# Windowed attention with a gated FFN on one core: DMA transposes issued one chunk earlier, loads reordered, a mask built on VectorE

## The chip, the core and the metric

The kernel runs on one core of a Trainium2 chip. The metric is the device time of one execution in microseconds (us). A profile is one execution recorded by the hardware profiler; its span is 1.7 to 1.8 us shorter than the time of the same run. Engines are called TensorE (PE in the profile, PEld for its weight loads), VectorE (DVE), ScalarE (ACT), GpSimd (POOL) and SP, which only issues DMAs here. In profile lines, `qn` and `kn` are q and k of a chunk as loaded, `qT` and `kT` the same transposed, `xb` the attention output and `xT` its transpose, `uu` and `hT` VectorE's two steps of the gate, `ost` a piece of output before its store, and `ps` a bank of PSUM, which the matmuls here write to.

## The reference, cut to what matters

Attention with 8 batches, 8 heads, 576 positions and head size 64; a query sees the 64 latest keys, itself included. Its output is laid out as 4608 tokens x 512 and goes through a gated FFN with 1536 inner columns.

```python
rel = pos[:, None] - pos[None, :]
mask = (rel >= 0) & (rel < 64)
scores = np.where(mask, scale * q @ k.T, -1e9)
attn = softmax(scores)
x = (attn @ v) as (4608, 512)
g = x @ w_gate
out = (g / (1 + exp(-g)) * (x @ w_val)) @ w_out
```

## The kernel before

The tokens are worked through in 36 chunks of 128 for attention and 9 chunks of 512 for the FFN. Every operation is recorded in program order, and the waits are derived from what it reads and writes. The parts that matter, cut and slightly simplified:

GpSimd issues all loads, in program order. q and k of chunk n go to one of 6 buffers, so a load waits until the chunk 6 back has been transposed. q and k of chunks 4 to 7 are transposed by TensorE (`T`), those of chunk 8 and later by DMA transposes that SP issues (`TD`). The attention output `xb` is transposed for the FFN in the same two ways (`X`, `XD`).

```python
W(2, 4)
self.init_mask(self.mask, "mask", 0.0)       # 4 selects on GpSimd
self.init_va(4, self.NV, "pool")             # 6 memsets on GpSimd
for f in range(4, 12, 2):
    W(f, f + 2)                              # W slices, gate and value
for n in range(4, 8):
    load(n)                                  # q, k, v of chunk n
...
for f in range(6):
    self.F(0, f, 256, 512)
self.T(4)                                    # TensorE needs q, k of chunk 4
...
self.S(8)
self.TD(10)
self.O(0, 0)                                 # ends in an output store on SP
...
def block(n):
    load(n + 5)
    self.A(n, n + 1)                         # attention of n, with the scores S(n + 1) inside
    if n != 11:
        self.XD(n)                           # xb -> xT by DMA transpose
    self.TD(n + 3)                           # q, k of chunk n + 3 by DMA transpose
```

Blocks 8 to 11 fall into FFN chunk 1. The first matmuls of FFN chunk 2, `F(2, 0)`, need xT of chunks 8 to 11; that of chunk 11 is made by TensorE.

The softmax here doesn't subtract the row's maximum and nothing guards it: scores larger than these inputs give would overflow.

Of the kernel before, what the change touches and what calls it, by code (L numbers as in the profile page):

```python
# [5 lines left out]
ALU = mybir.AluOpType  # L6
# [4 lines left out]
NCH = T // 128  # L11
# [138 lines left out]
class _Kernel:  # L150
# [70 lines left out]

    def init(self):
        g = self.g
        ident, mask = self.ident, self.mask
        g.op("dve", lambda e: e.memset(self.wz[:, :], 0.0), writes=["wz"])  # L225
        g.op("dve", lambda e: e.memset(ident[:, :], 0.0), writes=["ident"])  # L226
        g.op("dve", lambda e: e.memset(self.nmask[:, :], 0.0), writes=["nmask"])
        g.op("dve", lambda e: e.memset(mask[:, :], 1.0), writes=["mask"])
        g.op("dve", lambda e: e.memset(self.wup[:, :], 0.0), writes=["wup"])
        g.op("act", lambda e: e.activation(self.wup[:, :], self.wup[:, :], ACTF.Exp), writes=["wup"])  # L230
        g.op("dve", lambda e: e.memset(self.kT[:, :, 0:64], 0.0), writes=[("kT", -1, p) for p in range(4)])
        self.init_va(0, 4)

    def init_va(self, i0, i1, eng="dve"):
        g = self.g
        for i in range(i0, i1):
            va = self.va[i]
            g.op(eng, lambda e, va=va: e.memset(va[:, :, 64:80], 1.0), writes=[("va", i)],
                 after=[self.last_sel] if eng == "pool" else [])

    def init_pool_a(self):
        ident = self.ident
# [1 line left out]
            out=ident[:, :], in_=ident[:, :], compare_op=ALU.not_equal, fill=1.0, base=0,  # L244
            pattern=[[-1, 128]], channel_multiplier=1), writes=["ident"])

    def init_mask(self, m, key, fill):
        for p0, c0, op in ((0, 0, ALU.is_ge), (0, 64, ALU.is_gt), (64, 0, ALU.is_gt), (64, 64, ALU.is_ge)):
            d = m[p0:p0 + 64, c0:c0 + 64]
            sg = 1 if op == ALU.is_gt else -1  # L250
            self.last_sel = self.g.op("pool", lambda e, d=d, op=op, sg=sg: e.affine_select(  # L251
                out=d, in_=d, compare_op=op, fill=fill, base=0,
                pattern=[[-sg, 64]], channel_multiplier=sg), writes=[key])

    def load_qk(self, n):
        i = n % self.NQ
# [317 lines left out]
    def build(self):  # L574
        W = lambda a, b: (self.load_w("g", a, b), self.load_w("v", a, b))

        def load(n):
            if n < NCH:
                self.load_qk(n)
                self.load_v(n)  # L580

        self.first_loads()
        self.init()
        self.load_v(0)
        self.init_pool_a()
        self.load_v(1)
        self.init_mask(self.nmask, "nmask", -30000.0)
        W(0, 1)
        self.load_qk(2)
        W(1, 2)  # L590
        self.load_qk(3)
        self.load_v(2)
        self.load_v(3)
        W(2, 4)
        self.init_mask(self.mask, "mask", 0.0)
        self.init_va(4, self.NV, "pool")
        for f in range(4, 12, 2):
            W(f, f + 2)
        for n in range(4, 8):
            load(n)  # L600

        self.banks("a", [5, 6, 7, 4, 0, 1])
        self.warm(13)
        self.first_cast("k", None, "dve")
        self.first_cast("q", 0, "act")
        self.first_cast("q", 1, "dve")
        tk = self.first_T("k")
        tq = self.first_T("q")
        b0, b1 = self.bias(0), self.bias(1)
        for n in range(2):  # L610
            self.first_ev("k", n, "dve", *tk)
            self.first_ev("q", n, "act", *tq)
        self.S(0, b0)
        self.S(1, b1)
        self.warm(4)
        self.A(0)
        self.warm(2)
        self.A(1)
        self.warm(1)
        self.X(0, "act")  # L620
        self.warm(3)
        self.X(1, "act")
        self.warm(2)
        self.banks("a", [5, 6, 7, 4])
        self.F(0, 0, 0, 256)
        self.F(0, 1, 0, 256)
        self.T(2, "dve")
        self.T(3, "dve")
        load(8)
        b2 = self.bias(2)  # L630
        self.S(2, b2)
        b3 = self.bias(3)
        self.S(3, b3)
        self.F(0, 2, 0, 256)
        self.A(2)
        self.A(3)
        self.F(0, 3, 0, 256)
        self.X(2, "act")
        self.F(0, 4, 0, 256)
        self.X(3, "act")  # L640
        self.F(0, 5, 0, 256)
        self.load_wo(0, 6)
        self.load_wo(6, 12)
        load(9)

        for f in range(6):
            self.F(0, f, 256, 512)
        self.T(4)
        load(10)
        self.F(0, 6)  # L650
        self.S(4)
        self.T(5)
        load(11)
        self.F(0, 7)
        self.A(4, 5)
        self.F(0, 8)
        self.T(6)
        load(12)
        self.X(4, "act")
        self.F(0, 9)  # L660
        self.A(5, 6)
        self.F(0, 10)
        self.T(7)
        self.X(5, "act")
        self.F(0, 11)
        self.A(6, 7)
        self.TD(8)
        self.F(1, 0, 0, 256)
        self.F(1, 1, 0, 256)
        self.X(6, "act")  # L670
        self.F(1, 2, 0, 256)
        self.A(7)
        self.TD(9)
        self.F(1, 3, 0, 256)
        self.F(1, 4, 0, 256)
        self.X(7, "act")
        self.F(1, 5, 0, 256)
        for f in range(3):
            self.F(1, f, 256, 512)
        self.S(8)  # L680
        self.TD(10)
        self.O(0, 0)
        for f in range(3, 6):
            self.F(1, f, 256, 512)

        def block(n):
            if n >= NCH:
                return
            load(n + 5)
            self.A(n, n + 1 if n + 1 < NCH else None)  # L690
            if n != 11:
                self.XD(n)
            if n + 3 < NCH:
                self.TD(n + 3)

        place = {(1, 1, 2): 8, (1, 2, 0): 9, (1, 2, 1): 10, (1, 3, 0): 11,
                 (2, 0, 0): 12, (2, 1, 0): 13, (2, 1, 2): 14, (2, 2, 1): 15, (2, 3, 0): 16}
        for n in range(17, NCH):
            place[(n - 5) // 4, (n - 5) % 4, 0] = n
        for c in range(1, NFC):  # L700
            for u in range(int(c == 1), 4):
                late = c == NFC - 1 and u == 3
                for s in range(3):
                    if (c, u) != (1, 1):
                        self.F(c, 3 * u + s)
                    if s != 1 and (c, u, s) in place:
                        block(place[c, u, s])
                    if s == 1 and not late:
                        self.O(c - 1, u)
                    if s == 1 and (c, u, s) in place:  # L710
                        block(place[c, u, s])
                    if (c, u, s) == (1, 3, 1):
                        self.X(11, "act")
                if late:
                    self.O(c - 1, u)
        for u in range(3):
            self.O(NFC - 1, u)
        self.O_last(NFC - 1, 3)
        self.g.emit()
# [42 lines left out]
```

## Time and profile before

The kernel before took 347.3 us (median of 3, 346.23 to 348.19).

| stretch of the profile | what TensorE does |
|---|---|
| 0 to 31 us | first chunks, short gaps |
| 31.4 to 34.5 | waits for k of chunk 4 |
| 34.8 to 38.2 | works at half clock |
| 79.0 to 84.15 | waits for qT of chunk 11 |
| 84.15 to 89.4 | works at half clock |
| 97.6 to the end | FFN chunk 2 and later, busy throughout: 249.44 us |

The page divides the span into 40 slices; each digit is a busy share in tenths, and PEclk is the granted TensorE clock. From the page of the kernel before:

```profile
PE   6986998994999999999999999999999999999996
...
PEclk9999899997899999999999999999999999999999
DMA  9999999999999999999999999992333211100012
```

After the first quarter TensorE has no gap. The DMA engines are full for the first 27 slices. The gaps by their releaser, from the view of TensorE's waits (engine, line, what it waited for: us in total, times, longest):

```profile
PE ps L394 <- DMA qT<-qn: 5.1, 1, 5.1
PE ps L350 <- DMA kn<-in_k_dram: 3.0, 1, 3.0
...
PE ps L394 <- ACT ost L544: 0.9, 2, 0.4
PE ps L508 <- DVE uu L516: 0.6, 1, 0.6
```

L394 are the matmuls of the scores, L350 TensorE's transposes of q and k, L508 the first matmuls of the FFN (one line lower each in the changed kernel). Two waits hold nearly all of it. Around them, the busy times in stretches of 2 us (columns: PE, PEld, DVE, ACT, POOL busy, granted clock, DMA share, GB/s):

```profile
34.00:36.00 2.00, 1.54 (x11) 0.99 (x12) 0.00 (x0) 0.75 (x2) 2.00 (x4) 0.70 2.43 159
36.00:38.00 2.00, 2.00 (x7) 0.61 (x5) 0.42 (x1) 0.93 (x2) 2.00 (x4) 0.50 2.43 155
...
82.00:84.00 2.00, 0.00 (x0) 0.00 (x0) 0.00 (x0) 0.00 (x0) 0.00 (x0) 0.65 1.53 152
84.00:86.00 2.00, 1.85 (x43) 1.19 (x44) 0.87 (x4) 1.08 (x2) 1.65 (x2) 0.50 1.39 161
86.00:88.00 2.00, 2.00 (x6) 0.70 (x5) 1.42 (x4) 0.60 (x1) 2.00 (x4) 0.50 1.46 150
```

Each of these two waits costs its own time and then a stretch at half clock, in which TensorE shows as fully busy but does about half the work: four matmuls of 512 columns take 1.78 to 1.91 us there, and 1.03 at full clock. The chain of waits shows why qT of chunk 11 came so late (start, duration, what):

```profile
66.67 8.82 DMA kn<-in_k_dram
75.49 8.57 DMA qT<-qn
84.06 0.09 issue
84.15 0.59 PE ps L394 x10
```

The transpose was issued at 75.49 and landed at 84.06. Late in the kernel, where the DMA engines have little to do, the same transpose lands about 2.5 us after its issue.

### The profile page before, as it was taken

Reading aid. Unit: us, or ns where it says so; the run is one execution under the profiler, and the core shown is the slowest. Engines: PE = TensorE matmul, PEld = TensorE weight load, DVE = VectorE, ACT = ScalarE, POOL = GpSimd, SP = SyncE. Lnnn points to the kernel's source line nnn. Section 1 sums busy time; section 2 is a strip of 40 time slices with the busy share of each in tenths; the row PEclk is TensorE's granted clock in tenths of the full one; section 3 lists DMA queues with packets and bytes.
Section 4 is the critical chain, followed back from the end, with each engine's and each line's share of the span. In section 5 each row is a group of like instructions: output and inputs, shape, how many; then the busy total and the mean of one; then the engine's idle time right before and its main releaser. Section 6 shows DMA issues by size and latency. Waiting matters only on the chain.

```text
span 347.1 us, 8322 instructions
## 1 busy us (share of the span) xinstructions
PE 330.0 (95%) x3489; PEld 166.4 (48%) x3489; DVE 212.6 (61%) x465; ACT 139.2 (40%) x252; POOL 112.7 (32%) x151
## 2 busy tenths in 40 slices
PE   6986998994999999999999999999999999999996
PEld 3565457642444444444444444444444444444444
DVE  4366489661666676666666666666666666555520
ACT  2562674441344454444444444444444442232321
POOL 7999995322363436333331633300000000000000
PEclk9999899997899999999999999999999999999999
DMA  9999999999999999999999999992333211100012
GB/s 173 146 179 178 155 202 141 152 190 153 158 105 123 152 135 149 132 130 121 129 118 119 125 130 126 127 122 77 77 77 77 60 47 52 55 30 32 31 47 105
DMA packets 169909, 40.26 MB, mean 116 GB/s; under 512 B 156432, under 2 KB 165392, under 8 KB 169872
## 3 DMA queue, kind: packets, MB, share of 16 engines
q0 software_dynamic: 117312, 18.36, 76.0%
q1 hardware_dynamic: 51376, 20.72, 30.9%
q10 hardware_dynamic: 1184, 0.66, 0.7%
q8 instruction: 27, 0.44, 0.5%
q14 instruction: 10, 0.08, 0.1%
HBM read 37.75 MB, written 9.44 MB: 136 GB/s over the span
## 4 chain that ended last, share of the span: by engine, by line
PE 75%; POOL 11%; DMA 10%; issue 3%; DVE 0%; ACT 0%; POOLq 0%
PE ps L508 45%; PE ps L532 24%; DMA qn<-in_q_dram 5%; PE ps L443 3%; POOL va L325 3%; DMA kn<-in_k_dram 3%; DMA qT<-qn 2%; POOL kn L263 2%; PE ps L394 2%; POOL qn L263 2%; POOL Wv L331 2%; POOL Wg L331 2%; PE ps L561 1%; POOL Wo L336 0%; POOL nmask L251 0%
## 5 line engine op out<-in xcount | busy, mean ns | idle before, releaser
L516 DVE SCALAR_TENSOR_TENSOR uu<-sig,ps 128x512 bf16<-128x512 bf16 (+1 forms) x120 | 75.9, 632 | 91.9 <-ACT sig L514 91.7
L508 PE MATMUL ps<-xT,Wg 128*128 128x512 bf16 (+1 forms) x480 | 115.6, 364 | 0.9 <-DVE uu L516 0.6
L508 PE MATMUL ps<-xT,Wv 128*128 128x512 bf16 (+1 forms) x480 | 114.6, 362 | 0.4 <-DMA Wv<-in_moe_w_val_dram 0.4
L532 PE MATMUL ps<-Wo,hT 128*128 128x512 bf16 x420 | 95.9, 379 | 0.0
L514 ACT ACTIVATE sig<-ps 128x512 bf16<-128x512 f32 (+1 forms) x120 | 66.6, 555 | 62.6 <-PE ps L508 62.2
L518 DVE SCALAR_TENSOR_TENSOR hT<-uu,ps 128x512 bf16<-128x512 bf16 (+1 forms) x120 | 76.0, 634 | 4.9 <-PE ps L508 0.8
L508 PEld LDWEIGHTS ps<-xT,Wv 128*128 128x128 bf16 x480 | 47.2, 99 | 48.5 <-issue 2.2
L263 POOL DMA_DIRECT2D qn<-in_q_dram x38 | 34.3, 915 | 105.6 <-DMA qT<-qn 105.3
L532 PEld LDWEIGHTS ps<-Wo,hT 128*128 128x128 bf16 x420 | 41.0, 98 | 49.1
L508 PEld LDWEIGHTS ps<-xT,Wg 128*128 128x128 bf16 x480 | 44.1, 99 | 42.5 <-issue 2.2
L544 ACT ACTIVATE ost<-ps 128x512 f32<-128x512 f32 x35 | 20.9, 597 | 95.9 <-PE ps L532 95.9
L404 ACT ACTIVATE pt<-ps 128x512 bf16<-128x512 f32 x72 | 38.9, 595 | 29.3 <-PE ps L394 28.7
L325 POOL DMA_DIRECT2D va<-in_v_dram x40 | 36.4, 919 | 1.7 <-DVE ident L226 0.8
L263 POOL DMA_DIRECT2D kn<-in_k_dram x38 | 34.6, 915 | 3.1 <-DMA Wo<-in_moe_w_out_dram 3.1
L461 DVE TENSOR_TENSOR xb<-ps,rc 128x256 bf16<-128x256 f32 x72 | 30.6, 425 | 2.5
L409 DVE TENSOR_TENSOR pt<-pt,mask 128x512 bf16<-128x512 bf16 x64 | 24.2, 417 | 0.5 <-ACT pt L404 0.4
L443 PE MATMUL ps<-va,pt 64*64 64x65 bf16 x1088 | 23.0, 197 | 0.6 <-DVE pt L409 0.2
L443 PEld LDWEIGHTS ps<-va,pt 64*64 64x64 bf16 x1088 | 15.3, 107 | 15.8 <-issue 11.2
L458 DVE RECIPROCAL rc<-ps 128x4 f32<-128x4 f32 x72 | 12.6, 175 | 15.6 <-PE ps L443 15.6
L394 PE MATMUL ps<-qT,kT 64*64 64x64 bf16 (+1 forms) x864 | 16.1, 203 | 6.0 <-DMA qT<-qn 5.1
L394 PEld LDWEIGHTS ps<-qT,kT 64*64 64x64 bf16 x864 | 12.8, 109 | 8.5 <-issue 7.0
L311 PE MATMUL ps<-wz 128*128 128x512 bf16 x25 | 7.8, 446 | 1.3 <-DVE wz L225 1.3
(44 smaller groups left out, 62.8 us busy)
## 6 DMA issues: line engine op xcount, KB each, us to landing
out_dram<-ost SPq DMA_DIRECT2D x35, 256.0 KB, 2.5
va<-in_v_dram POOLq DMA_DIRECT2D x32, 128.0 KB, 6.2
qn<-in_q_dram POOLq DMA_DIRECT2D x30, 128.0 KB, 4.5
kn<-in_k_dram POOLq DMA_DIRECT2D x30, 128.0 KB, 6.0
Wo<-in_moe_w_out_dram POOLq DMA_DIRECT2D x2, 768.0 KB, 14.0
Wg<-in_moe_w_gate_dram POOLq DMA_DIRECT2D x5, 256.0 KB, 6.3
Wv<-in_moe_w_val_dram POOLq DMA_DIRECT2D x5, 256.0 KB, 7.1
fq<-in_q_dram ACTq DMA_DIRECT2D x1, 512.0 KB, 6.0
```

The costliest lines, as they stand in the source:

```text
L263: self.g.op("pool", lambda e, d=d, a=a: e.dma_start(d, a), writes=ks, dma=True)
L325: g.op("pool", lambda e, d=d, a=a: e.dma_start(d, a), writes=ks, dma=True)
L394: r = e.matmul(sv[h][o:o + 64, c, q0:q1], self.kT[ps, c, kk:kk + 64], qT[ps, c, q0:q1], start=not biased, stop=not biased or c == 3 and kk ...
L404: g.op("act", lambda e, po=po, si=si: e.activation(po, si, ACTF.Exp, scale=SCALE), reads=[bk], writes=[pk])
L409: "dve", lambda e: e.tensor_tensor(po, po, m, ALU.mult), reads=[pk, "mask"], writes=[pk]))
L443: r = e.matmul(av[half][ws, j, :], pt[ks, h, ws], vv[ks, h, 0:65], start=key == q[0], stop=key == q[-1])
L461: g.op("dve", lambda e, xo=xo, rb=rb, a=av[half]: e.tensor_tensor(xo, a[:, :, 0:64], rb, ALU.mult), reads=[bk, ("rc", ir)], writes=[("xb", ...
L508: r = e.matmul(bank[:, 0:n], W[:, kk, f * 128:f * 128 + 128], xT[:, kk, t0:t1], start=(kk == 0), stop=(kk == NK - 1))
L514: g.op("act", lambda e: e.activation(sig[:, 0:n], G[:, 0:n], ACTF.Tanh, scale=0.5), reads=[gk], writes=[("sig", i)])
L516: g.op("dve", lambda e: e.scalar_tensor_tensor(uu[:, 0:n], sig[:, 0:n], 1.0, G[:, 0:n], ALU.add, ALU.mult), reads=[("sig", i), gk], writes ...
L518: g.op("dve", lambda e: e.scalar_tensor_tensor(hT[:, f, t0:t1], uu[:, 0:n], 0.5, V[:, 0:n], ALU.mult, ALU.mult), reads=[("uu", i), vk], wr ...
L532: r = e.matmul(OB[:, :], hT[:, f, 128 * u:128 * u + 128], self.Wo[:, f, :], start=(f == 0), stop=(f == NF - 1))
```

## The change

Its intent: take away both waits. Loads of chunks 4 and 5 go between the W slices. Chunk 11 is transposed right after chunk 10, ahead of the output stores, and each block transposes four chunks ahead instead of three, with loads six ahead. The multiplicative mask comes from the additive one by one comparison on VectorE, and the six memsets move there too, which frees GpSimd for issuing loads.

```diff
-        self.init_va(0, 4)
+        self.init_va(0, self.NV)
...
-    def init_mask(self, m, key, fill):
+    def init_mask(self):
...
+        self.g.op("dve", lambda e: e.tensor_scalar(self.mask[:, :], self.nmask[:, :], -1.0, None, ALU.is_ge),
+                  reads=["nmask"], writes=["mask"])
...
-        W(2, 4)
-        self.init_mask(self.mask, "mask", 0.0)
-        self.init_va(4, self.NV, "pool")
-        for f in range(4, 12, 2):
+        for f in range(2, 8, 2):
             W(f, f + 2)
-        for n in range(4, 8):
-            load(n)
+        self.load_qk(4)
+        W(8, 10)
+        self.load_v(4)
+        load(5)
+        W(10, 12)
+        load(6)
+        load(7)
...
         self.TD(10)
+        load(13)
+        self.TD(11)
         self.O(0, 0)
...
-            load(n + 5)
+            load(n + 6)
...
-            if n + 3 < NCH:
-                self.TD(n + 3)
+            if n + 4 < NCH:
+                self.TD(n + 4)
```

(All ten memsets of `init_va` are on VectorE now. `init_mask` builds the additive mask on GpSimd as before and then derives the other. The memset of the old mask and the arguments that are no longer used go too.)

More of the change, by code (lines that the diff above doesn't have):

```diff
@@ L223, in init @@
         g = self.g
-        ident, mask = self.ident, self.mask
+        ident = self.ident
         g.op("dve", lambda e: e.memset(self.wz[:, :], 0.0), writes=["wz"])
@@ L227, in init @@
         g.op("dve", lambda e: e.memset(self.nmask[:, :], 0.0), writes=["nmask"])
-        g.op("dve", lambda e: e.memset(mask[:, :], 1.0), writes=["mask"])
         g.op("dve", lambda e: e.memset(self.wup[:, :], 0.0), writes=["wup"])
@@ L231, in init, with init_va @@
         g.op("dve", lambda e: e.memset(self.kT[:, :, 0:64], 0.0), writes=[("kT", -1, p) for p in range(4)])
-        self.init_va(0, 4)
-    def init_va(self, i0, i1, eng="dve"):
-        g = self.g
+        self.init_va(0, self.NV)
+    def init_va(self, i0, i1):
         for i in range(i0, i1):
             va = self.va[i]
-            g.op(eng, lambda e, va=va: e.memset(va[:, :, 64:80], 1.0), writes=[("va", i)],
-                 after=[self.last_sel] if eng == "pool" else [])
+            self.g.op("dve", lambda e, va=va: e.memset(va[:, :, 64:80], 1.0), writes=[("va", i)])
     def init_pool_a(self):
@@ L245, in init_pool_a @@
             pattern=[[-1, 128]], channel_multiplier=1), writes=["ident"])
-    def init_mask(self, m, key, fill):
+    def init_mask(self):
         for p0, c0, op in ((0, 0, ALU.is_ge), (0, 64, ALU.is_gt), (64, 0, ALU.is_gt), (64, 64, ALU.is_ge)):
-            d = m[p0:p0 + 64, c0:c0 + 64]
+            d = self.nmask[p0:p0 + 64, c0:c0 + 64]
             sg = 1 if op == ALU.is_gt else -1
-            self.last_sel = self.g.op("pool", lambda e, d=d, op=op, sg=sg: e.affine_select(
-                out=d, in_=d, compare_op=op, fill=fill, base=0,
-                pattern=[[-sg, 64]], channel_multiplier=sg), writes=[key])
+            self.g.op("pool", lambda e, d=d, op=op, sg=sg: e.affine_select(
+                out=d, in_=d, compare_op=op, fill=-30000.0, base=0,
+                pattern=[[-sg, 64]], channel_multiplier=sg), writes=["nmask"])
+        self.g.op("dve", lambda e: e.tensor_scalar(self.mask[:, :], self.nmask[:, :], -1.0, None, ALU.is_ge),
+                  reads=["nmask"], writes=["mask"])
     def load_qk(self, n):
@@ L586, in build @@
         self.load_v(1)
-        self.init_mask(self.nmask, "nmask", -30000.0)
+        self.init_mask()
         W(0, 1)
```

## The prediction

> **What bounds it.** The span is 347.1 us. From about 90 us to the end TensorE is the limit: the table by stretch shows it busy in practically every microsecond, and the chain of waits is matmuls alone. The change removes no TensorE work, so it can only gain before 90 us. There the waits of TensorE show two stalls worth naming:
>
> 1. 3.0 us at 31.4-34.5, waiting for kn of chunk 4. Its load is queued behind all W slices; loads of that stage come about 9 us after their issue, in issue order, so it is throughput of the DMA engines that decides, not issue time. The granted clock is 0.5 for 3.4 us afterwards (0.70 and 0.50 in the 2 us stretches from 34), which costs about 1.7 us more. Together 4.7.
> 2. 5.1 us at 79.0-84.15, waiting for the DMA transpose qT of chunk 11, issued at 75.5 and landed at 84.06: 8.6 us under a full load queue, where the same transpose late in the kernel takes about 2.4. The clock is 0.5 until 89.5, another 2.7. Together 7.8 to 7.9.
>
> The Trainium skill ("TensorE: Matmul & The Clock Gate", Part 1) gives half rate after an idle window of about 3.4 us; this trace agrees, the 0.6 us gap at 54 us cost no clock.
>
> **What the change does.** The order of loads: of the W slices, four loads (8 to 11, about 1.35 us of queue each) go behind chunk 4's q and k, so these should land near 29 instead of 34.4; stall 1 goes. But the queue's total is the same: chunk 5's k (near 34.4) and chunk 6's k (near 39.5, unmoved) are now wanted near 34.2 and 38.9 by a TensorE that is 4.7 us earlier. I leave 0.7 us of stall there.
>
> Chunk 11's transposes move from behind block 8 to behind chunk 10's: issued when kn lands, near 63.7, landed near 71-73, wanted near 74.3. Stall 2 goes. Chunk 12's (landed near 78) are wanted near 78.5, and chunk 10's xT (near 84) by the first matmuls of FFN chunk 2, near 84: no slack. "DMA: Bandwidth & Descriptors" (Issuing engines are not separate DMA queues) says that all queues share the 16 engines; the trace agrees: transposes and loads interleave there from 61 to 96 us. I leave 1 us of new stalls, too short to halve the clock.
>
> "Loads six ahead" changes little by itself: the GpSimd queue has the same order of loads and is held by the buffers' readers (105 us of waits for qT), so earlier transposes free it.
>
> Mask on VectorE: takes 2.1 us of GpSimd time (15.2-17.3), adds under 1 us of VectorE memsets near 2 us, where it waits for fk until 5.9. The DMA queue is 5 us behind issue there, so I count 0.
>
> **Sum.** 347.3 - (4.7 - 0.7) - (7.9 - 1.0) = 336.4 us. Range 333.9 to 340.5. Chances: faster 0.88, same 0.11, slower 0.01.
>
> **What would show it.** TensorE's wait for kn near 31 us under 1 us, no half clock after it; no 5 us wait for qT, no half clock near 84; the part from block 12 on unchanged in length, starting about 11 us earlier; the landing of Wo (54.8) unmoved.
>
> **What would make it wrong.** If transposes are held by their share of the engines rather than by latency, chunk 12's qT or chunk 10's xT lands 3 to 5 us late, and the stall moves there and takes the clock with it: 340 to 342. If chunk 5 or 6 lands later than I think, 1 to 2 us come back. If nothing of this binds, 334.5.

## The result, and the profile after

The changed kernel took 338.77 us (median of 4, 338.6 to 339.25), against 347.75 beside it. Ratios here are the mean time of one kernel's runs over that of the other's of the same rounds, so not quite the ratio of the medians quoted: 0.9751, 95% interval 0.9717 to 0.9785. The span is 337.0 us, against 347.1. From its page (its PE row; this trace holds no record of the clock, and that of a second profile of the same kernel, shown below it, stays at full):

```profile
PE   7989989999899999999999999999999999999996
```

```profile
PEclk9999999999999999999999999999999999999999
```

TensorE's waits of the changed kernel:

```profile
PE ps L507 <- DVE hT L517: 1.3, 1, 1.3
PE ps L393 <- ACT ost L543: 1.3, 3, 0.4
...
PE ps L507 <- DVE uu L515: 0.6, 1, 0.6
...
PE ps L393 <- DMA qT<-qn: 0.2, 1, 0.2
```

Both long waits are gone, and a new one of 1.3 us stands at the head of the list. The same stretches as before around the first one, and the new gap:

```profile
34.00:36.00 2.00, 2.00 (x27) 1.15 (x17) 1.70 (x4) 1.84 (x4) 2.00 (x4) 1.00 1.74 182
36.00:38.00 2.00, 2.00 (x55) 1.10 (x54) 1.22 (x2) 1.78 (x4) 2.00 (x4) 1.00 2.38 156
...
86.00:88.00 2.00, 0.69 (x4) 0.22 (x3) 1.38 (x2) 0.04 (x1) 1.00 (x2) 1.00 1.76 154
```

TensorE does the same matmuls in the same order in nearly all kernels, so two positions serve as a ruler: M1, the start of the transposes of xb of chunk 6 (just after the first stage), and M3, the start of `F(2, 0)`. Both are read from the traces.

| kernel | M1 | M1 to M3 | M3 to end | span |
|---|---|---|---|---|
| before | 53.81 | 43.81 | 249.44 | 347.1 |
| changed | 49.06 | 38.52 | 249.43 | 337.0 |
| changed, once more | 49.01 | 38.78 | 249.44 | 337.2 |

The last part is the same to 0.01 us: the whole change in span happens before M3, 4.75 us in the first part and 5.29 in the second.

### The profile page after: what moved, and what is told of

Its sections match the earlier page's. It is cut to its first block, busy times and chain, and to the rows that moved or that the text cites. A ratio compares the mean times of both kernels' runs of the same rounds, so it can differ in the third digit from the quotient of the medians.

```text
span 337.0 us, 8332 instructions
## 1 busy us (share of the span) xinstructions
PE 326.7 (97%) x3489; PEld 165.2 (49%) x3489; DVE 213.3 (63%) x471; ACT 139.1 (41%) x252; POOL 111.0 (33%) x141
## 4 chain that ended last, share of the span: by engine, by line
PE 85%; DMA 5%; POOL 4%; DVE 2%; ACT 1%; issue 1%; SPq 0%; POOLq 0%
PE ps L507 52%; PE ps L531 26%; PE ps L442 3%; DMA Wv<-in_moe_w_val_dram 3%; DMA qT<-qn 3%; PE ps L393 2%; POOL Wg L330 1%; POOL va L324 1%; PE ps L560 1%; POOL Wv L330 1%; DVE uu L515 1%; PE ps L349 1%; ACT ost L543 1%; POOL qn L262 1%; POOL kn L262 1%
## 5 line engine op out<-in xcount | busy, mean ns | idle before, releaser
L507 PE MATMUL ps<-xT,Wg 128*128 128x512 bf16 (+1 forms) x480 | 113.3, 359 | 2.2 <-DVE hT L517 1.3
L507 PE MATMUL ps<-xT,Wv 128*128 128x512 bf16 (+1 forms) x480 | 113.0, 358 | 0.3 <-DMA Wv<-in_moe_w_val_dram 0.2
## 6 DMA issues: line engine op xcount, KB each, us to landing
kn<-in_k_dram POOLq DMA_DIRECT2D x30, 128.0 KB, 10.2
```

Of the source, the lines that this page charges most:

```text
L507: r = e.matmul(bank[:, 0:n], W[:, kk, f * 128:f * 128 + 128], xT[:, kk, t0:t1], start=(kk == 0), stop=(kk == NK - 1))
```

## The experiments

Twelve kernels ran, each with runs of the kernel before on the same chip; all results were correct. The ruler for them:

| run | median us | before beside it | ratio (95%) | M1 | M1 to M3 |
|---|---|---|---|---|---|
| e1_loads | 343.34 | 347.77 | 0.9884 (0.9844 to 0.9924) | 50.17 | 43.32 |
| e2_td | 343.1 | 347.77 | 0.9849 (0.9795 to 0.9904) | 55.16 | 37.88 |
| e3_gate | 344.42 | 347.77 | 0.9902 (0.9856 to 0.9949) | 52.07 | 39.39 |
| e4_poolmask | 339.77 | 347.77 | 0.9781 (0.9742 to 0.982) | 50.23 | 38.26 |
| e6_td11_only | 340.77 | 346.87 | 0.9805 (0.977 to 0.984) | 48.98 | 40.70 |
| e7_x10 | 337.12 | 346.87 | 0.9705 (0.9676 to 0.9734) | 49.06 | 36.88 |
| e8_xd10_first | 337.1 | 346.87 | 0.9709 (0.9676 to 0.9743) | 48.78 | 37.16 |
| e10_warm | 344.8 | 346.87 | 0.9926 (0.989 to 0.9962) | 52.65 | 41.06 |
| e13_after_again | 338.41 | 346.81 | 0.9757 (0.9723 to 0.979) | 49.01 | 38.78 |
| e11_mask_late | 339.09 | 346.81 | 0.9773 (0.974 to 0.9806) | 48.94 | 38.70 |
| e12_mask_only | 345.44 | 346.81 | 0.9972 (0.9929 to 1.0015) | 53.05 | 43.80 |
| e5_load5_late | 342.01 | 346.81 | 0.9853 (0.9808 to 0.9898) | 52.54 | 37.96 |

One question needed no run. "Loads six ahead" with `load(n + 5)` in the blocks, and without the explicit `load(13)`, builds to the same instructions in the same order on every engine as the changed kernel. GpSimd has no other work between loads, so where the load stands in the program changes nothing; the buffers' readers hold it.

### e1_loads: the order of loads alone

```diff
 # kernel before
-        for f in range(4, 12, 2):
+        for f in range(4, 8, 2):
             W(f, f + 2)
-        for n in range(4, 8):
-            load(n)
+        self.load_qk(4); W(8, 10); self.load_v(4); load(5); W(10, 12); load(6); load(7)
```

> The kernel before with the new order of loads alone (mask still on GpSimd, transposes as before). Theory: stall 1 goes with its clock penalty, and TensorE, SP and GpSimd all move about 4.7 us earlier, chunk 11's transposes included, so stall 2 stays as it is: about 342.8 us. Rival: the backlog of loads alone decides when qT of chunk 11 lands (84 us); then stall 2 grows by what stall 1 gave, and the time stays near 347.

343.34 us, as the theory had it. Of TensorE's waits in this run:

```profile
PE ps L394 <- DMA qT<-qn: 4.6, 1, 4.6
...
PE ps L350 <- DMA kn<-in_k_dram: 0.3, 1, 0.3
```

The first wait goes, the second stays, and M1 comes 3.6 us earlier. TensorE starts on qT of chunk 11 at 79.94 instead of 84.15, so the rival, a landing that stays at 84, is out. M1 is 1.1 us later than in the changed kernel, which has the same order of loads; e4 says why.

### e2_td: the earlier transposes alone

```diff
 # kernel before
         self.TD(10)
+        load(13)
+        self.TD(11)
         self.O(0, 0)
-            load(n + 5)
+            load(n + 6)
-            if n + 3 < NCH:
-                self.TD(n + 3)
+            if n + 4 < NCH:
+                self.TD(n + 4)
```

> The kernel before with the earlier transposes alone (chunk 11 ahead of the output stores, four ahead in the blocks). Theory: stall 1 stays (3.0 us and a clock of 0.5 for 3.4 us); stall 2 goes with its clock, 7.2 us; about 340.3, up to 341.6 if the wait for xT of chunk 10 that the changed kernel shows near 87 us comes too. Rival: the two parts need each other, and less than 5 us come: over 342.5.

343.1 us, from 340.85 to 344.22: the median is the rival's number, and the time alone would have decided for it. The profile decides otherwise. It has no wait for qT at all; M1 to M3 takes 37.88 us, 5.9 less than before, even less than in the changed kernel. What was lost lies in the first part: this run waited 3.6 us for k of chunk 4, and the half clock lasted 6.8 us (33.8 to 40.65, so it began within the wait), twice as long as after the first wait in the profile of before.

```profile
PE ps L350 <- DMA kn<-in_k_dram: 3.6, 1, 3.6
PE ps L508 <- DVE uu L516: 1.7, 2, 1.1
```

The second line holds the new wait near 93 us, 1.1 us here. The four runs order by their mean granted clock: 340.85 and 342.51 us at 1.00, 343.7 at 0.995, 344.22 at 0.99. So the two parts don't need each other. That the spread is the clock's is likely for most of it, but not shown: two runs at 1.00 differ by 1.66 us, and 1.00 also stands for profiled runs whose traces hold no record of the clock (the changed kernel, e3).

### e3_gate: is it the full load queue that makes a transpose late?

Nothing is transposed earlier; the load of chunk 14 waits for qT of chunk 11, which leaves the DMA engines a load of 0.3 to 0.6 from 72 to 78 us (the DMA share of the profile), against about 2 in the kernel before.

```diff
 # kernel before
-                self.load_qk(n)
+                self.load_qk(n, [self.last_td] if n == 14 else ())   # last_td: the latest qT transpose
```

> The kernel before, transposes and W slices as they were; only the first load of chunk 14 waits for the landing of qT of chunk 11, so that loads 14 to 16 do not fill the DMA engines from 72 to 84 us. Theory (a full load queue makes a transpose land 8 us after its issue): qT of chunk 11, issued near 75.5, lands within 4 us, stall 2 shrinks to under 1 us: about 340.5 to 341.5. Rival (the transposes are slow by themselves, or by what stands ahead of them on SP): the landing stays 7 to 9 us after the issue, and the time stays near 347 or grows because loads come later.

The view of DMA issues for the two transposes of chunk 11 (the last number is us from issue to landing), in this run and then in the kernel before:

```profile
kT<-kn SPq DMA_TRANSPOSE x1, 4.0
qT<-qn SPq DMA_TRANSPOSE x1, 3.1
```

```profile
kT<-kn SPq DMA_TRANSPOSE x1, 7.8
qT<-qn SPq DMA_TRANSPOSE x1, 8.6
```

That is the theory's answer: 3.1 us instead of 8.6, with the same things ahead of it on SP. Before the scores of chunk 11 TensorE waited only 0.44 us, for a PSUM bank. The time, 344.42, is worse than expected (340.5 to 341.5), because the loads that were held back started at 77 us, and qT of chunk 12, issued at 78.4 among them, landed at 84.6:

```profile
PE ps L394 <- DMA qT<-qn: 2.6, 1, 2.6
```

This one is chunk 12's. The wait moved one chunk on. The trace of e3 holds no record of the clock, but TensorE's pace shows full clock after both of its waits, of 2.63 and 2.57 us (1.03 us for four matmuls of 512 columns). It is the fastest of the four runs, 342.62 us; the other three have mean clocks of 0.99 and 0.995, so some half clock is in the median too. Holding loads back treats the cause, but only for as long as they are held; issuing transposes early leaves the queue full and gives them the time.

### e4_poolmask: the changed kernel with the mask back on GpSimd

```diff
 # changed kernel: init_va, init_mask and the mask's memset as in the kernel before
-        for f in range(2, 8, 2):
-            W(f, f + 2)
+        W(2, 4)
+        self.init_mask(self.mask, "mask", 0.0)
+        self.init_va(4, self.NV, "pool")
+        for f in range(4, 8, 2):
+            W(f, f + 2)
```

> The changed kernel with the mask and the six memsets back on GpSimd behind the slices W 2 and 3. Theory: the queue of loads is 5 us behind its issue there, so 2.1 us of GpSimd time cost nothing: 338.8, within 0.5. Rival: later issue delays every load after it by 2 us, and chunk 6, which lands just when it is wanted, stalls TensorE near 39 us: 340 to 341.

339.77 us: about 1 us slower than the changed kernel (ratio 0.9781 against 0.9751), between the two theories, and outside what I had expected. M1 is 1.2 us later. The intervals of the two ratios overlap; M1 is clearer: in the six traces with the new order of loads for chunks 4 to 7 and no early mask on GpSimd it lies from 48.78 to 49.06, in the two with it at 50.17 and 50.23 (e1, e4). TensorE waits for chunk 5, and then for 0.44 us more at chunk 6:

```profile
PE ps L350 <- DMA kn<-in_k_dram: 0.8, 1, 0.8
```

```profile
40.05 0.38 PE L350 MATMUL ps<-ident,kn 128*128 128x128 bf16 x4 [0.44 <-DVE xb L461]
```

The profile puts the second down to VectorE, but k of chunk 6 landed at 39.96. The two waits together are the 1.2 us.

So my reading that "the DMA queue is 5 us behind issue" was wrong. The packets show it. In the kernel before, the first W load after the 2.1 us gap was issued at 17.28 and, counting packets in order, had its first one at 19.58, 2.3 us later. Thirteen later loads of that kernel found nothing queued ahead of them on GpSimd, and their first packets still came 1.4 to 1.6 us after the issue, their landing 3.3 to 4.3 us after it (97.52, 99.10 and 100.97 for the first of them). So the 5 us from issue to landing were mostly the latency of a load and its own transfer; some 0.7 us were queue. In the changed kernel the corresponding load waited 4.4 us (15.09 to 19.47), so the queue was some 2.8 us there, and the gap used it up but for 0.7. The rate dropped 5 us after the gap: in all six traces with the mask on GpSimd near 15 us it is 136 to 158 GB/s from 22 to 24 us, in the other eight 197 or 198. That the mask there causes the drop is thus shown; why it comes so late, and with 0.7 us still queued, is not. The stretch from 22 to 24 us, in the kernel before, this run and the changed kernel, in that order (last column: GB/s):

```profile
22.00:24.00 2.00, 1.92 (x61) 1.63 (x62) 1.86 (x8) 0.38 (x1) 2.00 (x4) 1.00 1.28 151
```

```profile
22.00:24.00 2.00, 1.59 (x29) 1.20 (x30) 1.86 (x8) 0.38 (x1) 2.00 (x4) 1.00 1.21 136
```

```profile
22.00:24.00 2.00, 1.93 (x61) 1.47 (x58) 1.86 (x8) 0.38 (x1) 2.00 (x4) 1.00 1.45 198
```

### e12_mask_only: the mask on VectorE alone

The kernel before with the new `init_va` and `init_mask`, and nothing else.

> The kernel before with the mask on VectorE alone. Theory: loads after 17 us land about 1 us earlier, so the wait for kn of chunk 4 is about 2 us instead of 3, with the clock as before: about 1 us faster than before, 346 where before is 347. Rival: the queue hides it, no change.

345.44 us against 346.81, a ratio of 0.9972 whose interval includes 1: by time alone no difference is shown. The rate from 22 to 24 us is 197 GB/s, as the theory has it, and the wait for chunk 4 is 0.8 us shorter than before's 3.0, with M1 0.8 us earlier. That shorter wait is no proof by itself: e2 and e3, with the loads of before, waited 3.6 and 2.6 us.

```profile
PE ps L349 <- DMA kn<-in_k_dram: 2.3, 1, 2.3
```

### e11_mask_late: the same GpSimd work where the queue is deep

```diff
 # e4_poolmask
-        self.init_mask(self.mask, "mask", 0.0)      # from behind W(2, 4)
-        self.init_va(4, self.NV, "pool")
...
         load(5)
+        self.init_mask(self.mask, "mask", 0.0)
+        self.init_va(4, self.NV, "pool")
         W(10, 12)
```

> The changed kernel with the mask and memsets back on GpSimd, but 11 us later than before had them: behind chunk 5's loads, near 26 us. Theory (a gap in the issues costs only where loads wait less for the engines than the gap is long): near 15 us a load lands 5 us after its issue, of which some 4 are there without any queue, and the gap of 2 us cost 1 us; near 26 us loads land 9 us after their issue, so the same gap costs nothing: as the changed kernel beside it, within 0.4, and no dip of the DMA rate near 22 or 31 us. Rival (GpSimd time delays all that comes after it, wherever it is): 0.8 to 1 us slower than the changed kernel, as when the mask stood near 15 us.

The dip is gone (198 GB/s from 22 to 24 us, and 150 near 31 us against 151 in the changed kernel), no load is waited for, and M1 is 48.94 us, as in the changed kernel (49.01 beside it). So for the stage in question the gap costs nothing there. The times don't quite follow: 339.09 against 338.41, 0.7 us apart where at most 0.4 was expected, while the two profiled spans are 337.1 and 337.2. The intervals of the two ratios overlap widely. I leave the remainder open.

### e13_after_again: the changed kernel once more

> The changed kernel once more, unedited, as the measure for the three runs beside it on the same chip: 338.8, within 0.5.

338.41 us (338.13 to 339.02, five runs), as expected. Its profile has the new wait at 1.6 us.

### e5_load5_late: only chunk 4 between the W slices

```diff
 # changed kernel
-        load(5)
         W(10, 12)
+        load(5)
```

> The changed kernel with chunk 5's loads back behind all W slices; only chunk 4 stays between them. Theory: kn of chunk 5 lands 2.7 us later, near 36.2, wanted near 34: a wait of about 2 us, and in some runs a slow clock after it: 340.5 to 342.5. Rival: chunk 4 alone was the stall, and the rest has slack: 338.8.

342.01 us, within the theory's range. The wait moved to chunk 5, and a half clock follows it (0.59 in the stretch from 36 us):

```profile
PE ps L349 <- DMA kn<-in_k_dram: 2.1, 1, 2.1
```

```profile
36.00:38.00 2.00, 1.97 (x12) 1.14 (x13) 0.00 (x0) 1.08 (x2) 2.00 (x4) 0.59 2.43 155
```

Once chunk 4 is early, chunk 5 is next in line: each move of a load must be judged with TensorE where it will then be, not where it was.

### e6_td11_only: chunk 11 early, the rest three ahead as before

```diff
 # changed kernel
-            if n + 4 < NCH:
-                self.TD(n + 4)
+            if 11 < n + 3 < NCH:
+                self.TD(n + 3)
```

> The changed kernel with only chunk 11's transposes early: from block 9 on each block issues the transposes of three chunks ahead, as before. Theory: a transpose under the load queue lands 7 to 9 us after its issue, so qT of chunk 12, now issued near 74 instead of 70.8, lands near 82 and is wanted near 79: a new wait of 1.5 to 3 us for it; xT of chunk 10 is issued 2 to 3 us earlier on a freer SP and its wait of 1.3 us goes: 338.5 to 341. Rival: chunk 11 alone mattered and four ahead is an ornament: no wait for qT, 337.5.

340.77 us, within the theory's range. qT of chunk 12 was issued at 73.7 instead of 70.8 and landed at 81.2:

```profile
PE ps L393 <- DMA qT<-qn: 2.2, 1, 2.2
```

Half clock followed for 3.4 us, and the wait near 87 us did not come. Four ahead is needed, for chunk 12.

### e7_x10 and e8_xd10_first: what is the new wait of 1.3 us?

The profile puts it down to VectorE's `hT`. In the timeline of the changed kernel, TensorE starts just as that instruction ends (start, duration, engine, line, what):

```profile
85.24 1.03 PE L507 MATMUL ps<-xT,Wv 128*128 128x512 bf16 x4
...
86.79 0.69 DVE L517 SCALAR_TENSOR_TENSOR hT<-uu,ps 128x512 bf16<-128x512 bf16 x1
87.47 1.19 SPq L362 DMA_TRANSPOSE kT<-kn  x1
...
87.58 1.02 PE L507 MATMUL ps<-xT,Wg 128*128 128x512 bf16 x4 [1.31 <-DVE hT L517]
```

But the DMA transpose of chunk 10's xb landed at 87.38, and these matmuls read it. SP had issued it only at 78.8: chunk 13's two transposes stood ahead of it, and the second held SP from 75.6 to 78.1. Two ways to take that away:

```diff
 # e7_x10: changed kernel, xT of chunk 10 made by TensorE and ScalarE
-            if n != 11:
+            if n not in (10, 11):
                 self.XD(n)
...
+                    if (c, u, s) == (1, 2, 2):
+                        self.X(10, "act")
```

> The changed kernel with xT of chunk 10 made by TensorE and ScalarE, as that of chunk 11 is, instead of by a DMA transpose. Theory: the wait of 1.3 us near 86 us, which the profile puts down to VectorE, is the wait for this transpose (landed 87.4); it goes, against some 0.3 us of TensorE for the four transposes: 337.7. Rival: it is VectorE's hT or a PSUM bank: 338.8 to 339.2.

```diff
 # e8_xd10_first: changed kernel, chunk 13's transposes behind chunk 10's xT
+            if n == 9:
+                return
+            if n == 10:
+                self.TD(13)
             if n + 4 < NCH:
                 self.TD(n + 4)
```

> The changed kernel with the transposes of chunk 13 moved on SP from behind block 9 to behind the DMA transpose of chunk 10's xT in block 10. Theory: SP was held by chunk 13's two transposes (its qT issue took 2.5 us), so xT of chunk 10 is issued near 76 instead of 78.8 and lands near 84, before it is wanted at 86.3; the wait of 1.3 us goes and nothing is added on TensorE: 337.4; chunk 13 is wanted near 87 and lands near 86. Rival: the landing is set by the load queue and not by the issue, and it lands near 87 all the same: 338.8.

337.12 us (337.01 to 337.17) and 337.1 (336.74 to 338.07): both faster than the changed kernel by 1.3 to 1.7 us (338.41 and 338.77; these two did not run beside it), and neither has the wait. In e8 the DMA transpose was issued at 76.3 and landed at 83.7, and TensorE goes on before VectorE's `hT` has even begun:

```profile
85.94 1.03 PE L507 MATMUL ps<-xT,Wg 128*128 128x512 bf16 x4
86.59 0.74 PEld L507 LDWEIGHTS ps<-xT,Wv 128*128 128x128 bf16 x4
86.63 0.69 DVE L517 SCALAR_TENSOR_TENSOR hT<-uu,ps 128x512 bf16<-128x512 bf16 x1
```

The wait was for the DMA transpose; the name in the profile was that of the engine that happened to finish last. In e8 the part from M3 to the end is 249.72 us, 0.28 longer than elsewhere: qT of chunk 13, now behind, landed at 88.14, and its scores start at 88.18. e7, with the narrower spread, is the version to keep: 0.9705 of before.

### e10_warm: waits filled with work, nothing moved

```diff
 # kernel before
             self.F(0, f, 256, 512)
+        self.warm(12)                       # matmuls on zeros
         self.T(4)
...
+            if n == 10:
+                self.warm(22)
             self.A(n, n + 1)
```

> The kernel before with nothing moved: 12 matmuls on zeros (about 0.22 us each) ahead of the transposes of chunk 4 and 22 ahead of block 10, so that TensorE works through most of both waits and its clock stays at full. Theory: each wait costs its own time and then a clock of 0.5 for one or two steps of 3.4 us; the second part goes here, 1.7 to 3.4 us and 2.7 to 3.4 us: 342 to 344, and a narrower spread than before's 346 to 349. Rival: the slow clock hides under other waits and costs nothing; then the time is 347 or more.

344.8 us against 346.87, at the upper end of what was expected, and the four runs lie within 0.44 us (before: 346.21 to 348.65 in its seven). The clock stayed at full. So some 2 us (1.3 to 3.8 by the interval of the ratio) is the least that the half clock cost in the kernel before; the zeros also made TensorE late, as the run waited 1.2 us for a bank ahead of the first of them and had no wait left for chunk 4. This shows the second cost of a wait apart from its first.

## Why the prediction was right, and where its sizes were off

The change made the kernel faster, and the time, 338.77 us, lies in the range of 333.9 to 340.5. It is 2.4 us above the point, 336.4. Point by point:

- **Both named waits were the gain, and nothing after them changed.** Right: both are gone with their half clocks, and from M3 on the two traces agree to 0.01 us.
- **First part: 4.7 less 0.7.** It gave 4.75. The 0.7 of "stall there" did not come, and the reason is the term that the prediction put at zero: "The DMA queue is 5 us behind issue there, so I count 0". Latency was taken for a queue. Without the mask's move chunks 5 and 6 are waited for (e4, 1.2 us in all); with it chunk 5's k landed at 33.55 instead of the expected 34.4 and chunk 6's at 38.75 instead of 39.5. For the same reason the second half of Wo, named as unmoved, landed 1 us earlier (53.76 instead of 54.80; 54.81 in e4). The order of loads alone gave 3.64 (e1), 0.36 less than predicted, and the mask's move some 1.1 more: by luck the two errors partly cancel.
- **Second part: 7.9 less 1.0.** It gave 5.29. Matching TensorE's matmuls one by one in the two traces, the lead grows from 4.75 at M1 to 11.9 at most, so the wait with its clock was worth 7.2, not 7.9: of the 5.1 us, 0.44 stands for a PSUM bank and is there in the changed kernel as well, and the rest of the difference was not placed. Then 1.9 is lost again, not 1.0: 0.4 to qT of chunk 12 (landed 79.28; predicted 78) and 1.48 at `F(2, 0)`, where xT of chunk 10 landed at 87.38 (predicted 84). The prediction named both places. Issued as soon as its input was there, that transpose lands at 83.7 (e8), as predicted; what the prediction missed is that chunk 13's transposes stand in front of it on SP.
- **"Loads six ahead" does little by itself.** Right, more strictly than meant: it builds to the same instructions.
- **The base.** 10.9 us read from the profile were subtracted from the median of 347.3, but the profiled run took 348.78. In profiles the error is 0.8 us (10.9 against 10.1). The rest, 1.5 us, is this. The profiled run had 10.2 us of half clock; of the 25 runs of the kernel before beside the experiments, ten had its mean clock of 0.985 and fifteen 0.99 or 0.995, which come to some 7 or 3.5 us. For the three runs behind the median the clock isn't on record, so that it makes the difference there is likely and not shown.

The Trainium skill's "DMA: Bandwidth & Descriptors" (Issuing engines are not separate DMA queues) says that DMAs of all issuers share 16 engines and interleave. The runs agree and give the size: a transpose took 8.6 us to land beside a full load queue, and 3.1 without it. What the prediction said of the half clock, that this trace agrees with an idle window of about 3.4 us, holds only roughly: in the kernel before a wait of 3.05 us was enough, and in e5 and e6 waits of 2.06 and 2.20 us brought it on.

## What to carry to other kernels

When a wait is removed, recompute when each later input is wanted with the engine where it will then be: here chunk 5, chunk 12 and chunk 10's xT each became the next limit by turns. Before calling work on a DMA-issuing engine free, compare a load's delay to its first packet with that of a load on an empty queue; time to landing by itself doesn't tell a queue from latency. Where the gap comes close to the queue, as here, only a run tells. And subtract a saving read in a profile from that profiled run, not from a median of runs with less of the loss in them.

## What the Trainium skill lacked or had wrong

- "TensorE: Matmul & The Clock Gate" (Part 1: The HAM clock gate) puts the half rate after "≥1 idle window (~3.4µs)", and its rules name gaps over about 3 us. Here waits of 2.06 us (e5) and 2.20 us (e6) were followed by it, two of 2.63 and 2.57 us in e3 were not (by TensorE's pace), and none of up to 1.57 us was (e13). That the window is free-running, as the page says, fits a wait that sometimes triggers and sometimes doesn't; but a wait of 2.06 us can't hold a whole idle window of 3.4, so why 2 us can be enough is not there.
- The same page reckons, in its case of DMA waits within a kernel (HAM oscillation), with 1.67 us at half clock for each. Here it comes in steps of 3.41 us, the window that the page gives: 3.41 and 6.83 in the profile of before. The kernel before spread over 345.08 to 349.23 us in eleven runs, with mean clocks of 0.995 (the fastest), 0.99 (345.93 to 347.19) and 0.985 (347.79 to 349.23). The kernels without a wait of 2 us or more spread over 0.2 to 1.7 us.
- "DMA: Bandwidth & Descriptors" (Latency and other measured facts) gives about 1 us to the first byte for a DMA issued by GpSimd and doesn't say from where it counts. Here, with nothing queued ahead on GpSimd, the first packet came 1.4 to 1.6 us after the start of the issue and 0.7 to 0.8 after its end (13 loads of the kernel before, from 97.52 us on), and the landing 3.3 to 4.3 us after the start.
- No page gives the latency of a DMA transpose beside loads. Here it was 8.6 us to landing under a full queue and 3.1 without; and the first packets of chunk 11's kT came 5.2 us after the issue (changed kernel, 62.05 to 67.25, with chunk 10's transposes still ahead of it on SP), against 1.2 late in the kernel before.
- No page warns that a wait put down to a compute engine can be one for a DMA that landed shortly before: 1.3 us "for VectorE" were the DMA transpose of xT (e7, e8).
